# A delta-rule attention with expert layer on one core: weight conversion, first queries and the start of the order are changed

## The chip, the core and the metric

The kernel runs on one core of a Trainium2 chip. The core has a matrix engine (TensorE; PE in the profile, its weight loads PEld), a vector engine (VectorE, DVE), a scalar engine (ScalarE, ACT), a general engine (GpSimd, POOL) and a queue engine (SyncE, SP) that issues transfers. The metric is the device time of one execution in microseconds; a comparison states medians over several runs.

## What is computed

Two steps, the second fed by the first. The first is a recurrence over 768 positions for 4 x 8 = 32 heads of 48 channels, the second a two-layer network over the 3072 resulting rows:

```python
k_n = k / (norm(k) + 1e-06)
for t in range(S):
    y[t] = q[t] @ state
    v_old = state.T @ k_n[t]
    state = state + beta[t] * outer(k_n[t], v[t] - v_old)
h = y @ w_in                       # 384 -> 2048
g = h * tanh(softplus(h))
out = g @ w_out                    # 2048 -> 384
```

q, k, v and beta are float32. The two weight matrices are float64.

## The kernel before

The recurrence is cut into 12 chunks of 64 positions. Within a chunk the products of keys with keys (the "gram") are formed, a triangular system is solved, and the chunk's outputs and the next state follow from small products. The names of the stages are those of the tiles in the profile.

- `early(g)` prepares two chunks at a time. Keys are loaded into `ksrc`, turned in 32x32 blocks by VectorE (`kt`, L408), multiplied (`pg`, L425), masked into `d` (L433) and turned again (`gt`, L451). Then come the norms (`root`, L464), the scaling with beta (L493) and the solve by forward steps, two VectorE operations each (L514, L515). Between the scaling and the end of the solve, GpSimd sets the diagonal of `gt` to one (L504). For the first two pairs of chunks (`split`) the solve covers blocks of 16 in 14 steps, and two products, `ma` (L557) and `mb` (L568), put the halves together. `tu` (L526), `tt` (L528) and `tn` (L576) are turned copies of the solution.
- `s_a` and `s_b` (tiles `ta`, `tb`) join the two 32-blocks of a chunk. `s_gq` multiplies keys and queries, and from chunk 1 on also keys and state (`gq`); VectorE masks the result (L713). `s_z` gives the corrected values (`pz`), `s_y` the outputs (`py`) and the next state (`ps`). All of their products are issued at L590. Each runs twice a chunk, for the two halves h of the heads.
- `turn_q` brings the queries of a chunk, loaded in pieces into `qsrc`, to the layout of the products: two VectorE block transposes for each half (L685). The working tiles `xx` hold state, queries, keys and an identity block; the identity blocks are copied there by VectorE (L278).
- `turn` transposes the outputs (`xt`, L799) and splits them into a high and a low part. `moe(n)` runs the network for chunk n: eight times an `up` product group (`h`, L824, 18 products of 256 columns), the activation on ScalarE (L839, L840, L841) and a `down` group (`acc`, L834, 12 products of 384 columns).
- `convert` turns each of 28 tiles of float64 weights, called parts, from pairs of 32-bit words to a high and a low 32-bit part. For each: ScalarE scales the upper word (L354); GpSimd writes the sign bit over the upper word (L358, two operations in one instruction, compare and multiply) and clamps (L361); VectorE joins in the remaining bits with two operations (L365); ScalarE rounds to the high part (L374); TensorE subtracts it for 24 of the parts (L379, L381) and ScalarE writes the low part (L383), for the others VectorE does both (L385). The temporaries come from the buffers `g`, `e`, `w` and two spare tiles, in the order of `TEMPS`.

The order is made when the kernel is built. Each piece of work is an `op` with an engine, an estimated duration, a priority (lower is earlier), the ops that it follows and the buffers that it holds. `Plan.run` walks forward in estimated time and picks, of what can start soonest, the op of the lowest priority; each engine then executes its instructions in that order. The priorities are set by constants (`SOON`, `E1`, `CV0` and others at L855). `Plan.feed` models how PE's instructions arrive. Semaphores are set by the framework from the data that the instructions share.

At the start SP loads keys, beta, three parts, the queries, two parts, values and keys again, then the other parts; a part from the sixth on waits until the one five before it was scaled (`AHEAD`, L898). `keep_warm` (L868) runs 76 products of zeros on PE before the first keys arrive.

Of the kernel before, what the change touches and what calls it, by code (L numbers as in the profile page):

```python
# [44 lines left out]
class Plan:  # L45
# [6 lines left out]
    THERE, PACKET, ASK, TAKES = 448, 256, 320, 4.0  # L52
# [12 lines left out]
    def feed(self, t, took, words, there, done):  # L65

        rate, left = words / took, words
        while True:
            while done is not None and done <= t:
                there += self.PACKET  # L70
                done = done + self.TAKES if there <= self.ASK else None
            if done is None and there <= self.ASK:
                done = t + self.TAKES
# [12 lines left out]
    def run(self):  # L86
# [12 lines left out]
        def when(o):  # L99
# [15 lines left out]
            if o.words:  # L115
                t = max(t, free["PE"])
                t = max(t, self.feed(t, o.took, o.words, there, due)[0] - o.took)
# [3 lines left out]
        while todo:  # L121
# [20 lines left out]
            if o.words:  # L142
                _, there, due = self.feed(t, o.took, o.words, there, due)
# [27 lines left out]
def kernel(  # L171
# [16 lines left out]
    P = 128  # L188
# [52 lines left out]
    def clear(engine, r0, *ts):  # L241
        for t in ts:
# [5 lines left out]
               op("POOL", 1.0, -100, lambda: [clear(nc.gpsimd, r0, qsrc) for r0 in (32, 96)])]  # L248
# [15 lines left out]
    made = op("POOL", 4.0, -200, constants, bufs=[ident0])  # L264
# [9 lines left out]

    def beside(t):
        for hh in range(2):
            r = slice(64 - 64 * hh, 128 - 64 * hh)
            nc.vector.tensor_copy(t[r, :, hh, D + C:], bcast_mid(ident[r, r.start:r.start + D], PB))  # L278

    eyes = [op("DVE", 0.6, -60, lambda t=t: beside(t), eyer) for t in xx]  # L280
# [5 lines left out]
    def load_src(dst, src, n, prio, *after, engine="SP"):  # L286
# [12 lines left out]
        return made  # L299

# [32 lines left out]
    def convert(k, got):  # L333
# [23 lines left out]
        def sign():  # L357
            nc.gpsimd.tensor_scalar(words()[:, :, 1], a(), 0.0, -2.0 ** 31, op0=ALU.is_lt, op1=ALU.mult)  # L358
# [8 lines left out]
        o = op("POOL", 0.1 + 0.6 * u, prio, sign, o, bufs=held)  # L367
        o = op("POOL", 0.1 + 0.6 * u, prio, clamp, o, bufs=held)
# [25 lines left out]

    kts, ats, nes, tns, vts, yys, ktd, tnd, ned, ttd = {}, {}, {}, {}, {}, {}, {}, {}, {}, {}
    mas = {}
    last_kt, last_s, solves, zs = {}, {}, {}, {}

    def early(g, at):
# [3 lines left out]
        for t2 in range(2):  # L403
# [23 lines left out]
            m = op("PE", 1.5 if g else 1.8, at(0.1 + 0.03 * t2), gram, ktd[n], bufs=[kt, *ps, dt, am], words=256)  # L427
# [76 lines left out]
        o = op("POOL", 0.15, at(0.26), lambda: nc.gpsimd.memset(gf()[:, ::33], 1.0), o, bufs=[gr])  # L504
        for j in range(1, sz - 1):
# [11 lines left out]
            o = op("DVE", 2 * (0.142 + nb_ * m * j * 0.00132), at(0.3 + 0.6 * j / sz), step, o, bufs=[gr, pr])  # L517
        tn = tns[g] = buf("tn", [P, 2, NP, 32], f"tn{g}")
# [143 lines left out]
    loaded, qdn, vdn, sdn, ydn, gdn, zdn, ptr = {}, {}, {}, {}, {}, {}, {}, {}  # L662
# [17 lines left out]
    def turn_q(n, h, prio, got):  # L680
# [6 lines left out]
        qdn[n, h] = op("DVE", 1.46, prio, turn, *got, cleared[4], ydn.get((n - 1, h)), gdn.get((n - 1, h)))  # L687

    def s_gq(n, h):
# [35 lines left out]
        return Stage(0.9 if n else 1.0, 64, products, [qdn[n, h], ktd[n], vdn[n, h], *sdn.get((n - 1, h), ())], [kt, *pg], outs)  # L725
# [137 lines left out]


    zero, warm = buf("e", [P, 512], "zero"), buf("h", [P, 512], "warm")
    o = op("DVE", 0.5, -230, lambda: nc.vector.memset(zero(), 0.0), bufs=[zero])

    def keep_warm():  # L868
        zb = zero().bitcast(BF16)
        for i in range(76):  # L870
            nc.tensor.matmul(warm()[0:32, 0:32] if i < 68 else warm(), zb[:, 0:32 if i < 68 else P], zb[:, :32 if i < 68 else 512],
                             start=True, stop=True)

    op("PE", 5.0, -210, keep_warm, o, bufs=[zero, warm], words=152)
# [7 lines left out]
    def loads(m, prio):  # L882
        for k in todo[:m]:
            kind, i = parts[k]
            got[k] = op("SP", 0.62, prio + 0.001 * k, lambda kind=kind, i=i: load_w(kind, i),
                        kb=1.25 if kind == "i" else 0.95)
        del todo[:m]

    loads(3, -99.5)
    q0 = load_src(qsrc, qq, 0, -99.4)  # L890
    loads(2, -99.3)
    for h in range(2):
        v0 = load_v(0, h, -99.2)
# [22 lines left out]
    mas[1].after += [ydn[0, h] for h in range(2)]  # L916
    for h in range(2):
# [46 lines left out]

    with tc.manual_schedule():
# [32 lines left out]
```

## Time and profile before

| | us |
|---|---|
| median of 3 runs | 646.54 |
| range of the runs | 645.41 to 646.61 |
| the profiled execution | 643.59 |
| its span | 641.8 |
| busy: PE, PEld | 591.0, 550.7 |
| busy: DVE, ACT, POOL | 423.1, 286.0, 150.4 |

The profile comes from one execution. Its span runs from the first to the last recorded event and lies 1.8 us below that execution's own time. Busy times count instructions in execution, so that a line of 92% for PE still says nothing of what PE waited for in a given stretch; the views by stretch, by line and in order of time do. The granted clock is the share of TensorE's full clock that the throttle allowed.

### The profile page before, as it was taken

To read this page: it belongs to the slowest core of one execution; us is meant where nothing else is said; L and a number is where in the kernel's file an instruction comes from. 1 tells how busy PE (TensorE), PEld (TensorE's weight loads), DVE (VectorE), ACT (ScalarE), POOL (GpSimd) and SP (SyncE) were. 2 spreads that over 40 slices of the span, in tenths; PEclk is the share of its full clock that TensorE was granted. 3 is DMA by queue.
4 is the path that set the end of the run, shared out by engine and by line. 5 is a ranking of instruction groups with operands and counts; after the bars stand their busy time and mean duration, and the time that the engine had idled before them with its cause. 6 is when DMAs were issued, how large, how long until landed. Compare 5 with 4: busy or idle time off the path is not lost.

```text
span 641.8 us, 23122 instructions
## 1 busy us (share of the span) xinstructions
PE 591.0 (92%) x10204; PEld 550.7 (86%) x10204; DVE 423.1 (66%) x888; ACT 286.0 (45%) x611; POOL 150.4 (23%) x140
## 2 busy tenths in 40 slices
PE   6049887988999999999999999999999999999996
PEld 4047666867989999999999999999999999999996
DVE  6859699887369984589893499864799932431110
ACT  2116764654553446444446533454433464343322
POOL 6992998795001001010020010010010100000000
PEclk9557989899999999999999999999999999999999
DMA  7886376002331314413115213133123121010001
GB/s 160 205 198 163 53 154 218 14 15 32 64 50 19 66 23 60 68 27 56 30 33 88 35 26 64 26 46 59 27 33 55 27 39 27 15 26 2 19 7 25
DMA packets 160932, 37.77 MB, mean 59 GB/s; under 512 B 154176, under 2 KB 157248, under 8 KB 160832
## 3 DMA queue, kind: packets, MB, share of 16 engines
q1 hardware_dynamic: 156160, 35.85, 28.7%
q8 instruction: 80, 1.31, 0.8%
q10 hardware_dynamic: 4672, 0.44, 0.5%
q14 instruction: 20, 0.16, 0.1%
HBM read 31.56 MB, written 4.72 MB: 57 GB/s over the span
## 4 chain that ended last, share of the span: by engine, by line
PE 79%; DVE 6%; POOL 4%; issue 2%; ACT 1%; POOLq 0%; DVEq 0%
PE h L824 31%; PE acc L834 30%; PE py L590 4%; PE gq L590 2%; PE pz L590 2%; PE ps L590 2%; PE pg L425 2%; POOL ri L358 1%; PE xt L799 1%; PE tb L590 1%; PE ta L590 1%; DVE mi L365 1%; POOL ro L358 1%; POOL mi L361 1%; DVE spare L365 1%
## 5 line engine op out<-in xcount | busy, mean ns | idle before, releaser
L824 PE MATMUL h<-x,wi 128*128 128x256 f32 x1728 | 226.4, 285 | 0.8 <-DVE x L803 0.8
L834 PE MATMUL acc<-wo,g 128*128 128x384 f32 x1152 | 223.7, 343 | 1.6 <-DVE g L841 1.6
L824 PEld LDWEIGHTS h<-x,wi 128*128 128x128 f32 x1728 | 215.3, 189 | 4.6 <-DVE x L803 1.0
L834 PEld LDWEIGHTS acc<-wo,g 128*128 128x128 f32 x1152 | 199.7, 189 | 4.9 <-DVE g L841 1.9
L841 DVE TENSOR_TENSOR g<-e,g 128x512 fp32r<-128x512 f32 x96 | 66.8, 696 | 118.0 <-ACT g L840 117.8
L839 ACT ACTIVATE e<-h 128x512 f32<-128x512 f32 x96 | 57.4, 598 | 172.0 <-PE h L824 153.5
L840 ACT CAST g<-e 128x512 fp32r<-128x512 f32 x96 | 59.7, 622 | 2.6
L515 DVE TENSOR_TENSOR gt<-gt,pr 128x84 f32<-128x84 f32 (+14 forms) x148 | 53.7, 363 | 5.1
L677 POOL TENSOR_TENSOR vt<-vt,ne 128x384 f32<-128x384 f32 x24 | 21.8, 921 | 137.8 <-DVE gt L515 46.8
L514 DVE TENSOR_TENSOR pr<-gt 128x84 f32<-128x84 f32 (+14 forms) x148 | 51.5, 348 | 3.2
L590 PEld LDWEIGHTS py<-xx 128*64 128x64 f32 x768 | 37.5, 142 | 5.7 <-issue 4.7
L713 DVE TENSOR_TENSOR xx<-gq,amask 64x256 f32<-64x256 f32 x96 | 40.5, 422 | 1.7
L590 PE MATMUL py<-xx 128*64 128x48 f32 x768 | 41.2, 228 | 0.4 <-issue 0.4
L504 POOL MEMSET gt<- 128x32 f32 x6 | 0.9, 158 | 166.0 <-DVE gt L493 166.0
L685 DVE STREAM_TRANSPOSE xx<-qsrc 64x512 f32<-64x512 f32 x48 | 33.9, 706 | 6.9 <-PE ps L590 3.7
L590 PE MATMUL ps<-xx 128*48 128x48 f32 x704 | 36.4, 208 | 1.2 <-issue 1.2
L706 DVE TENSOR_TENSOR vt<-vt,gq 64x192 f32<-64x192 f32 (+1 forms) x66 | 23.3, 352 | 19.6 <-PE gq L590 18.9
L779 ACT COPY yy<-py 128x384 f32<-128x384 f32 x24 | 11.5, 479 | 46.8 <-PE py L590 30.2
L609 ACT COPY xx<-pz 64x192 f32<-64x192 f32 x92 | 28.8, 313 | 7.7 <-PE pz L590 6.6
L590 PEld LDWEIGHTS ps<-xx 128*48 128x48 f32 x704 | 30.3, 125 | 2.0 <-issue 1.3
L590 PE MATMUL gq<-xx,kt 64*64 64x112 f32 (+1 forms) x768 | 31.0, 268 | 0.6 <-DVE at L632 0.6
L590 PE MATMUL pz<-vt,tt 64*64 64x48 f32 x768 | 27.8, 224 | 0.5 <-ACT tt L609 0.5
(113 smaller groups left out, 666.0 us busy)
## 6 DMA issues: line engine op xcount, KB each, us to landing
ri<-in_moe_w_in_dram SPq DMA_DIRECT2D x12, 512.0 KB, 6.4
ro<-in_moe_w_out_dram SPq DMA_DIRECT2D x16, 384.0 KB
vt<-in_v_dram SPq DMA_DIRECT2D x48, 96.0 KB, 5.7
xx<-in_k_dram SPq DMA_DIRECT2D x48, 96.0 KB, 3.0
out_dram<-o SPq DMA_DIRECT2D x48, 96.0 KB, 2.9
qsrc<-in_q_dram SPq DMA_DIRECT2D x48, 64.0 KB, 2.7
ksrc<-in_k_dram SPq DMA_DIRECT2D x44, 64.0 KB, 2.7
qsrc<-in_q_dram SPq DMA_DIRECT2D x48, 32.0 KB, 3.1
```

The costliest lines, as they stand in the source:

```text
L514: nc.vector.tensor_tensor(out=pv, in0=nj, in1=xj, op=ALU.mult)
L515: nc.vector.tensor_tensor(out=below, in0=below, in1=pv, op=ALU.add)
L590: nc.tensor.matmul(*a, start=True, stop=True)
L609: (nc.scalar.copy if e == "ACT" else nc.vector.tensor_copy)(out=a, in_=b)
L685: nc.vector.transpose(xx[h][r, :, hh, D:D + C], src)
L706: nc.vector.tensor_tensor(out=vt()[r, p4, :], in0=vt()[r, p4, :], in1=pg[h4]()[i, :, 0:D], op=ALU.subtract)
L713: nc.vector.tensor_tensor(out=x[r, p4, hh, D:D + C], in0=pg[h4]()[i, :, d:], in1=bcast_mid(amask[i], 4), op=ALU.mult)
L824: nc.tensor.matmul(h()[:, f2, :], wt["i", f * P // WI * NCH + c][:, i2, f0:f0 + P], x[:, c, :], start=(i == 0), stop=(i == 3 * NCH - 1))
L834: nc.tensor.matmul(acc[t]()[:, :DM], gg()[:, a, f2, ts_], wt["o", f][:, i2, :], start=(f == 0 and i == 0), stop=(f == NF - 1 and i == 2))
L839: m = op("ACT", 0.58, prio + 0.1, lambda e=e, h=h: nc.scalar.activation(e(), h(), AF.Mish, scale=-1.0), m, bufs=[h, e])
L840: m = op("ACT", 0.58, prio + 0.1, lambda e=e, gg=gg: nc.scalar.copy(out=gg()[:, 0], in_=e()), m, bufs=[e, gg])
L841: m = op("DVE", 0.7, prio + 0.1, lambda e=e, gg=gg: nc.vector.tensor_tensor(out=gg()[:, 1], in0=e(), in1=gg()[:, 0], op=ALU.subtract), m, ...
```

## The change

The conversion: the sign becomes one operation, the scaled number times zero, written as a float whose bits are the sign alone. The clamp now comes before it, and one clamp in four (parts k with k % 4 = 3) runs on VectorE.

```diff
         def sign():
-            nc.gpsimd.tensor_scalar(words()[:, :, 1], a(), 0.0, -2.0 ** 31, op0=ALU.is_lt, op1=ALU.mult)
+            nc.gpsimd.tensor_scalar(words()[:, :, 1].bitcast(F32), a(), 0.0, None, op0=ALU.mult)
-        def clamp():
-            nc.gpsimd.tensor_scalar(a(), a(), -F64_MOST * 2.0 ** -112, F64_MOST * 2.0 ** -112, op0=ALU.max, op1=ALU.min)
+        def clamp(engine):
+            engine.tensor_scalar(a(), a(), -F64_MOST * 2.0 ** -112, F64_MOST * 2.0 ** -112, op0=ALU.max, op1=ALU.min)
...
-        o = op("POOL", 0.1 + 0.6 * u, prio, sign, o, bufs=held)
-        o = op("POOL", 0.1 + 0.6 * u, prio, clamp, o, bufs=held)
+        o = op("POOL", 0.25 + 1.72 * u, prio, lambda: clamp(nc.gpsimd), o, bufs=held) if k in CLAMP_POOL else \
+            op("DVE", 0.13 + 0.3 * u, prio, lambda: clamp(nc.vector), o, bufs=held)
+
+        o = op("POOL", 0.15 + 0.9 * u, prio, sign, o, bufs=held)
```

The queries of chunks 0 and 1 are loaded in their own layout by two transfers (in place of eight), turned by products with the identity on TensorE, and copied by ScalarE. The blocks of `xx` that VectorE's transposes filled with zeros are cleared by GpSimd for this; the clearing of `qsrc` moves behind the reading of chunk 1.

```diff
+    def load_q(n, prio, *after):
+        return [op("SP", 0.6, prio, lambda hh=hh: load(qnat[64 * hh:64 * hh + 64], qq[hh, C * n:C * n + C]), *after, kb=0.9)
+                for hh in range(2)]
...
-        qdn[n, h] = op("DVE", 1.46, prio, turn, *got, cleared[4], ydn.get((n - 1, h)), gdn.get((n - 1, h)))
+        if n > 1:
+            qread[n, h] = op("DVE", 1.46, prio, turn, *got, cleared[4], ydn.get((n - 1, h)), gdn.get((n - 1, h)))
+            qdn[n, h] = [qread[n, h]]
+            return
+        ps = buf("ps", [P, PB, C], f"qt{n}_{h}")
+        x = xx[h]
+
+        def products():
+            for p in range(PB):
+                for hh in range(2):
+                    r = slice(64 * hh, 64 * hh + 64)
+                    nc.tensor.matmul(ps()[64 - 64 * hh:64 - 64 * hh + D, p, :], qnat[r, PB * h + p, :], ident[r, r], start=True, stop=True)
+
+        def out(hh):
+            r = slice(64 - 64 * hh, 64 - 64 * hh + D)
+            nc.scalar.copy(out=x[r, :, hh, D:D + C], in_=ps()[r])
+
+        m = qread[n, h] = op("PE", 1.0, prio, products, *got, eyer, ydn.get((n - 1, h)), gdn.get((n - 1, h)), bufs=[ps], words=64)
+        qdn[n, h] = [op("ACT", 0.62, prio, lambda hh=hh: out(hh), m, cleared[5], ydn.get((n - 1, h)), gdn.get((n - 1, h)), bufs=[ps])
+                     for hh in range(2)]
```

The identity blocks are copied by GpSimd, and the diagonal of the first two pairs is set by VectorE:

```diff
+    def clear_turned():
+        for t in xx:
+            for hh in range(2):
+                r0 = 96 - 64 * hh
+                nc.gpsimd.memset(t[r0:r0 + 32, :, hh, D:D + C], 0.0)
+
+    cleared.append(op("POOL", 2.2, -150, clear_turned))
...
-            nc.vector.tensor_copy(t[r, :, hh, D + C:], bcast_mid(ident[r, r.start:r.start + D], PB))
+            nc.gpsimd.tensor_copy(t[r, :, hh, D + C:], bcast_mid(ident[r, r.start:r.start + D], PB))
...
-        o = op("POOL", 0.15, at(0.26), lambda: nc.gpsimd.memset(gf()[:, ::33], 1.0), o, bufs=[gr])
+        e = "DVE" if split else "POOL"
+        o = op(e, 0.17, at(0.26), lambda: (nc.vector if split else nc.gpsimd).memset(gf()[:, ::33], 1.0), o, bufs=[gr])
```

Products of zeros, besides the 76 at the start, follow steps 2 and 8 of the first solve; their operand moves from the buffer `e` to `x0`.

```diff
+    def keep_warm(n, after, prio, few=0):
+
+        warm = buf("h", [P, 512], "warm")
+
+        def products():
+            for i in range(few + n):
+                m = 32 if i < few else P
+                nc.tensor.matmul(warm()[0:m, 0:4 * m], zero()[:, 0:m], zero()[:, 0:4 * m], start=True, stop=True)
+
+        op("PE", 0.03 * few + 0.4 * n, prio, products, after, bufs=[warm, zerob], words=2 * (few + n))
+
+    WARM = {2: 2, 8: 12}
+    keep_warm(8, o, -210, few=68)
...
             o = op("DVE", 2 * (0.142 + nb_ * m * j * 0.00132), at(0.3 + 0.6 * j / sz), step, o, bufs=[gr, pr])
+            if g == 0 and j in WARM:
+                keep_warm(WARM[j], o, -96)
```

The loads at the start come in another order: queries, values and keys of chunk 0 first, then eleven parts after the second gram, the others after the output product of chunk 0. `AHEAD` is gone.

```diff
-    loads(3, -99.5)
-    q0 = load_src(qsrc, qq, 0, -99.4)
-    loads(2, -99.3)
+    q0 = load_q(0, -99.5)
     for h in range(2):
-        v0 = load_v(0, h, -99.2)
+        v0 = load_v(0, h, -99.4)
         scale_v(0, h, -95, *v0)
-        kxd[0, h] = load_k(0, h, -99.1)
+        kxd[0, h] = load_k(0, h, -99.3)
+    loads(FIRST, -99.2, grams[1])
     loads(28, -99.0)
...
-    for k in range(AHEAD, len(parts)):
-        got[k].after.append(copied[k - AHEAD])
...
+    for k in range(FIRST, len(parts)):
+        got[k].after.append(ydn[0, 1])
```

The rest concerns the plan: other estimates for some durations (GpSimd's above all), another model of PE's instruction supply in `feed`, other priorities, and a low part by TensorE for 25 of the parts in place of 24.

```diff
-    SOON, SOON1, E1, EG, ES, LATE1, LATE = -0.13, 0.007, 0.17, -0.226, 1.8, 0.251, -0.137
-    E1S, LAG, PRIO_XT, CV0, CV1, G1A, XA = 0.646, 2.1, 0.479, -0.25, 1.238, 0.908, 0.14
-    LO_PE = range(24)
-    AHEAD = 5
+    SOON, SOON1, E1, EG, ES, LATE1, LATE = -0.13, 0.377, 0.281, -0.715, 2.034, 0.016, 0.173
+    E1S, LAG, PRIO_XT, CV0, CV1, G1A, XA = 0.898, 2.266, 0.735, -0.411, 1.156, 0.891, -0.134
+    LO_PE = range(25)
+    FIRST = 11
+    CLAMP_POOL = [k for k in range(len(parts)) if k % 4 < 3]
```

More of the change, by code (lines that the diff above doesn't have):

```diff
@@ L63, in op, with feed @@
         return o
-    def feed(self, t, took, words, there, done):
+    def feed(self, t, took, words, there, done, line):
         rate, left = words / took, words
         while True:
[L69 to L73, printed above, removed]
+            if done is not None and done <= t:
+                there, done = there + self.PACKET, None
+            if done is None and there <= self.ASK and left > 0:
+                done = t + self.TAKES + max(0.0, line - t)
             if left <= 0:
@@ L116, in when @@
                 t = max(t, free["PE"])
-                t = max(t, self.feed(t, o.took, o.words, there, due)[0] - o.took)
+                t = max(t, self.feed(t, o.took, o.words, there, due, line)[0] - o.took)
             return t
@@ L142, in run @@
             if o.words:
-                _, there, due = self.feed(t, o.took, o.words, there, due)
+                _, there, due = self.feed(t, o.took, o.words, there, due, line)
             if o.kb:
@@ L247 @@
                op("POOL", 0.5, -219, lambda: clear(nc.gpsimd, 96, ksrc1()), bufs=[ksrc1]),
-               op("POOL", 1.0, -100, lambda: [clear(nc.gpsimd, r0, qsrc) for r0 in (32, 96)])]
+               op("POOL", 1.3, 0.5, lambda: [clear(nc.gpsimd, r0, qsrc) for r0 in (32, 96)])]
+    qnat = qsrc.rearrange("p a b c -> p (a b c)")[:, :NP * D].rearrange("p (a d) -> p a d", d=D)
     def constants():
@@ L262, in constants @@
                                     channel_multiplier=-1)
-    made = op("POOL", 4.0, -200, constants, bufs=[ident0])
+    made = op("POOL", 2.9, -200, constants, bufs=[ident0])
     eyer = op("DVE", 0.3, -98, lambda: nc.vector.tensor_copy(identr, ident0()[:, 0:P]), made, bufs=[ident0])
@@ L277, in beside @@
             r = slice(64 - 64 * hh, 128 - 64 * hh)
-            nc.vector.tensor_copy(t[r, :, hh, D + C:], bcast_mid(ident[r, r.start:r.start + D], PB))
-    eyes = [op("DVE", 0.6, -60, lambda t=t: beside(t), eyer) for t in xx]
+            nc.gpsimd.tensor_copy(t[r, :, hh, D + C:], bcast_mid(ident[r, r.start:r.start + D], PB))
+    eyes = [op("POOL", 1.3, -60, lambda t=t: beside(t), eyer) for t in xx]
     def load(dst, src, queue="SP"):
@@ L392, in sides, with zero @@
         return [(slice(64 * i, 64 * i + 64), slice(64 - 64 * i, 128 - 64 * i)) for i in range(2)]
+    zerob = buf("x0", [P, NCH * UT], "zero")
+    def zero():
+        return zerob().bitcast(BF16)
+    o = op("DVE", 0.3, -230, lambda: nc.vector.memset(zero()[:, 0:512], 0.0), bufs=[zerob])
+    def keep_warm(n, after, prio, few=0):
[7 more added lines that the diff above has]
+    keep_warm(8, o, -210, few=68)
     kts, ats, nes, tns, vts, yys, ktd, tnd, ned, ttd = {}, {}, {}, {}, {}, {}, {}, {}, {}, {}
-    mas = {}
+    mas, grams = {}, {}
     last_kt, last_s, solves, zs = {}, {}, {}, {}
@@ L723, in outs @@
                          for h4 in range(2)]
-        return Stage(0.9 if n else 1.0, 64, products, [qdn[n, h], ktd[n], vdn[n, h], *sdn.get((n - 1, h), ())], [kt, *pg], outs)
+        return Stage(0.9 if n else 1.0, 64, products, [*qdn[n, h], ktd[n], vdn[n, h], *sdn.get((n - 1, h), ())], [kt, *pg], outs)
     def s_z(n, h):
@@ L862, in PRIO_CV @@
         return CV0 + CV1 * k / 28
[L865 to L874, printed above, removed]
     betas = load_beta()
@@ L963 @@
             solves[n // 2 + 1].after.append(m)
+    cleared[4].after += [qread[1, h] for h in range(2)]
     with tc.manual_schedule():
```

13 lines of the change are left out of this document (7 added, 6 removed).

## The prediction

> **What bounds the kernel now.** First the page (span and slices), then busy time by stretch, to see where the slack lies. The windows' columns are start:end, length, then busy us and instruction count of PE, PEld, DVE, ACT and POOL, the granted clock, the DMA share and GB/s.
>
> ```profile
> span 641.8 us, 23122 instructions
> POOL 6992998795001001010020010010010100000000
> ```
> ```profile
> 0.00:35.00 35.00, 9.89 (x332) 7.03 (x332) 26.00 (x63) 7.38 (x13) 28.28 (x40) 0.75 0.83 197
> 35.00:160.00 125.00, 105.68 (x2438) 87.06 (x2439) 101.66 (x192) 66.98 (x143) 96.00 (x65) 0.89 0.44 100
> 160.00:642.00 482.00, 475.44 (x7436) 456.65 (x7434) 295.44 (x635) 211.62 (x456) 26.13 (x37) 1.00 0.23 38
> ```
>
> From 160 us on PE is busy 475.4 of 482 us and POOL nearly idle: there the products set the end, and nothing in this change makes them fewer. So a gain is the amount by which the state of 160 us is reached sooner. Until then PE stands idle 25.1 + 19.3 us, at a mean clock of 0.75 and 0.89.
>
> The first 66 us are a chain from the first keys to the first expert product, as the timelines of PE and DVE show (start, duration, instruction, and in brackets the idle time before it and what ended it):
>
> ```profile
> 35.26 1.90 PE L557 MATMUL ma<-tu,d 16*32 16x16 f32 x128 [21.67 <-DVE tu L526]
> 41.42 1.68 PE L568 MATMUL mb<-tt,ym 32*32 32x16 f32 x110 [3.26 <-issue]
> 48.68 1.42 PE L590 MATMUL tb<-at,tn 32*32 32x32 f32 x64
> 50.61 2.49 PE L590 MATMUL pz<-vt,tt 64*64 64x48 f32 x64 [0.52 <-ACT tt L609]
> 53.03 3.03 PE L590 MATMUL py<-xx 128*64 128x48 f32 x64
> 66.56 2.30 PE L824 MATMUL h<-x,wi 128*128 128x256 f32 x18
> ```
> ```profile
> 7.26 3.12 DVE L278 COPY xx<-identr 64x384 f32<-64x384 f32 x4
> 10.30 1.22 DVE L408 STREAM_TRANSPOSE kt<-ksrc 128x1024 f32<-128x1024 f32 x1
> 32.72 1.27 DVE L520 TENSOR_TENSOR gt<-gt,bp 128x512 f32<-128x512 f32 x1 [1.70 <-POOL gt L504]
> 36.93 1.44 DVE L685 STREAM_TRANSPOSE xx<-qsrc 64x512 f32<-64x512 f32 x2
> 43.15 0.42 DVE L573 TENSOR_TENSOR tt<-tt,mb 128x256 f32<-128x256 f32 x1 [4.77 <-PE mb L568]
> 47.52 3.52 DVE L713 TENSOR_TENSOR xx<-gq,amask 64x256 f32<-64x256 f32 x8
> ```
>
> PE waits 21.67 us for the solve on DVE, then runs ma, mb, tb, pz and py with gaps between them; the first y is there at 56.06, the first expert product (h) starts at 66.56. From 60 to 160 us the weights are converted while all engines are nearly full:
>
> ```profile
> 60.00:160.00 100.00, 87.19 (x1750) 71.22 (x1739) 83.79 (x159) 59.50 (x126) 82.08 (x54) 0.97 0.37 88
> ```
> ```profile
> 62.10 1.92 POOL L358 TENSOR_SCALAR ro<-mo 128x384 int32<-128x384 f32 x1 [12.63 <-PE loi L381]
> ```
>
> The second row shows that POOL had stood idle for 12.63 us before that stretch: its temporaries were all held until PE and DVE came to the weights. The next three rows, busy time of one line over 0 to 160 us, are the sign (L358), the clamp (L361) and the two joins (L365):
>
> ```profile
> 0.00:160.00 160.00, 52.32 (x28) 0.86 0.53 121
> 0.00:160.00 160.00, 49.05 (x28) 0.86 0.53 121
> 0.00:160.00 160.00, 37.67 (x56) 0.86 0.53 121
> ```
>
> There are 28 parts (tiles of weights). Each costs POOL 1.87 us of sign and 1.75 us of clamp, and DVE 1.35 us for its two joins.
>
> **The change, part by part.** Times are against the profiled execution, 643.59 us: its span of 641.8 and 1.8 around it. The runs have a median of 646.54, 2.95 above it; the sum is a difference and I take it from that median.
>
> *Identity blocks to POOL.* The four copies (L278, 3.12 us) stand on DVE between the first and the second key transpose. How early could the second start? Its last keys leave on ACT's queue by 5.88 us and take 2.9 us:
>
> ```profile
> 0.84 5.04 ACTq L284 DMA_DIRECT2D ksrc<-in_k_dram  x8
> ```
> ```profile
> ksrc<-in_k_dram ACTq DMA_DIRECT2D x4, 32.0 KB, 2.9
> ```
>
> so about 8.8 where it is 10.30 now. **-1.5**, between 0 and -3.1. On POOL the copies and four more memsets lie in its idle time before the first weight. Only the SP loads of k into xx wait for them, and behind these the weight loads in SP's queue; the weights now also wait for the second gram. I expect them to leave about 3 us later than now, which costs nothing while POOL's first nine parts end before the chain does.
>
> *Diagonal memset to DVE (first two groups).* It waits 1.70 us behind the signs in POOL's queue; its own time is
>
> ```profile
> 32.53 0.16 POOL L504 MEMSET gt<- 128x32 f32 x1
> ```
>
> On DVE it costs about the same: **-1.5**, -1.0 at the least.
>
> *Products of zeros during the solve.* Two after step 2 and twelve after step 8. What they can win is the clock from ma to py. The same products at full clock, later in the trace:
>
> ```profile
> 58.98 1.26 PE L557 MATMUL ma<-tu,d 16*32 16x16 f32 x128
> 150.33 1.26 PE L568 MATMUL mb<-tt,ym 32*32 32x16 f32 x128
> 73.49 0.75 PE L590 MATMUL tb<-at,tn 32*32 32x32 f32 x64
> 585.70 0.68 PE L590 MATMUL pz<-vt,tt 64*64 64x48 f32 x32
> 592.88 1.14 PE L590 MATMUL py<-xx 128*64 128x48 f32 x32
> ```
>
> ma 0.64 shorter; mb 1.68 x 128/110 = 1.95 to 1.26, 0.7; tb 0.67 and ta, of the same count and size, as much; pz 2.49 to 2 x 0.68, 1.13; py 3.03 to 2 x 1.14, 0.75. Together **-4.6**, or 0 if the clock stays low. How the clock moves:
>
> ```profile
> 17.00:18.00 1.00, 0.00 (x0) 0.00 (x0) 0.91 (x3) 0.00 (x0) 1.00 (x1) 0.82 0.14 24
> 55.00:56.00 1.00, 1.00 (x33) 0.94 (x31) 0.96 (x2) 0.97 (x2) 0.00 (x0) 0.91 0.76 154
> 48.36:51.77 3.41, 2.81 (x104) 2.32 (x100) 3.21 (x9) 0.72 (x2) 1.04 (x2) 0.50 0.55 63
> 51.77:55.18 3.41, 3.41 (x86) 3.32 (x83) 3.22 (x8) 1.41 (x5) 0.00 (x0) 0.50 0.32 54
> 82.48:85.90 3.42, 1.56 (x129) 1.46 (x130) 3.32 (x6) 1.30 (x4) 3.26 (x3) 1.00 0.99 267
> 86.00:87.00 1.00, 1.00 (x3) 0.55 (x2) 1.00 (x3) 0.29 (x1) 1.00 (x1) 0.50 1.03 349
> ```
> ```profile
> L871 PE MATMUL warm<-zero 128*128 128x512 bf16 x8 | 3.6, 631 | 0.0
> ```
>
> A microsecond with a mean of 0.82 fell to 0.5 at 17.64, one with 0.91 rose at 55.18. After 3.4 us with PE 82% busy (48.36 on) it did not rise, after the next, fully busy, it did; after 3.4 us at 46% (82.48 on) it was low again. Eight products of the same size at the kernel's start take 3.6 us together (last row), 0.45 each, so twelve fill 5.4 us without a gap, and by the solve's own rows they end about 1 us ahead of ma: enough for one full stretch of 3.4 us in many cases, not in all. I take the gain, and keep the other case as a rival.
>
> The Trainium skill, page "TensorE: Matmul & The Clock Gate", Part 1, says that the clock is gated by a free-running window of 4096 cycles, 3.4 us, and that where the first products fall in it is chance. The trace agrees: 55.18 - 17.64 is 37.54 us, eleven times 3.41. By that rule alone a gapless 5.4 us holds a whole window in six of ten phases, and the sum would then be -4.6 in one execution and nearer 0 in the next.
>
> *Weight loads held back: eleven until the second gram, seventeen until the first y.* Ahead of mb, PE waits 3.26 us for nothing that the profile shows. PE's instructions come over a DMA queue of their own, through engines that weight loads keep full:
>
> ```profile
> q8 instruction: 80, 1.31, 0.8%
> ```
> ```profile
> ri<-in_moe_w_in_dram SPq DMA_DIRECT2D x12, 512.0 KB, 6.4
> ```
>
> Eleven parts are 5.1 MB: at the 197 GB/s of the first 35 us they last 26 us, past mb; at twice that, when short runs are out of the way, half as long. Between 0 and -3.3 I take **-2.0**. The other seventeen then start near 45 us and take 6.4 us each to land, several at a time; POOL still has parts of the eleven to do.
>
> *First queries by PE and ACT.* Four turns of 1.44 us leave DVE (two of them for chunk 1). PE gets 16 small products and ACT two copies for each, in idle time of both. The query products (gq) then no longer wait for the solve, and the masking (3.52 us on DVE) can fall into the 4.77 us in which DVE waits for mb. tb starts at 48.68 because gq is ahead of it on PE; at's copies are done where the masking begins, 47.52. **-1.2**; 0 to -2.4.
>
> So y(0) is there at 56.06 - (1.5 + 1.5 + 4.6 + 2.0 + 1.2) = 45.3.
>
> *From y(0) to the first expert product*: 10.5 us now, in which DVE does the joins of the first parts and PE the low halves. DVE has 2.9 us less of turns, can place joins in its gaps, and POOL no longer stops for lack of buffers as early. **-3**, between 0 and -7.
>
> *Sign by one operation, a quarter of the clamps on DVE.* The new sign is a one-operation TENSOR_SCALAR, which the trace lacks. Below stands a copy, above the two-operation form (1.87):
>
> ```profile
> L545 POOL COPY tt<-tt 32x512 f32<-32x512 f32 x24 | 15.9, 663 | 31.3 <-DVE tt L528 23.2 <-DVE tt L573 7.1
> ```
>
> I take half of the two-operation form, 0.95. POOL then has 28 x 0.95 + 21 x 1.75 = 63 us in place of 101; DVE gets seven clamps, whose nearest row is a join of the same size (0.67); I take 0.5, since a clamp reads one tensor: 3.5 us. The Trainium skill, "GPSIMD Engine Reference", section 3.1, puts a body of at most two operations at 1.03 cycles an element; by that a sign of 512 elements is an estimated 0.44 us and POOL's sum 49; no run here shows it. POOL was 82% busy in 60 to 160 and is not the limit after. What is late next is DVE (84%) or PE (87%): PE can gain at most its 12.8 us of idle time. I take **-5**, well under half, since the two have to be full together; 0 to -13.
>
> *Other order.* From 160 us on PE has 6.6 us of idle time, most of it the end's drain; I cost the new order there at nothing. The cover is PE's own queue; were it gone, each lost us is a us.
>
> Sum: 10.8 + 3 + 5 = **18.8 us**. Span 623.0, the profiled time 624.8, the runs 646.54 - 18.8 = **627.7**.
>
> **The rivals.**
> 1. *The clock stays low to py.* For it: one window at 82% did not raise it. Against: 5 us without a gap. 632.3. Chance 0.20.
> 2. *DVE becomes the bound.* After the first solve (36.93) DVE does 99.7 us of work by 160; less 5.8 of turns, plus 3.5 of clamps, 97.4. If it packs these no better than now (101.66 of 125, 81%), 120 us from 33.9 (36.93 - 3.0) give 154, a gain of 6: 640.5. For it: DVE waits little in that stretch. Against: part of its idle time was waiting for POOL and mb. 0.14.
> 3. *The sign in one operation is no shorter*, so that part does not do what it says: POOL keeps 52 + 37 us, the -5 and a third of the -3 go: 633.7. Against: every element meets one operation less. 0.07.
> 4. *PE is packed full*: g at -13, the wait before h at -7: 627.7 - 8 - 4 = 615.7. 0.12.
> 5. *Slower: the held loads starve the experts.* Seventeen parts land from about 51 us on and go through four temporaries. Now twenty parts take 62 to 150, 4.4 us each. From 5.9 us a part on, (152 - 51) / 17, the conversion ends later than today; at 6.5 PE loses some 9 us: 655. For it: each part crosses ACT, POOL, DVE, ACT, PE and ACT again. Against: POOL's share falls from 3.6 to about 2.3 us. 0.05.
>
> The forecast, gains of 14 to 24 us, has 0.42. The range 612 to 641 holds the forecast, rivals 1 and 3, most of 2 and 4, and leaves out 5 and the outer ends of 2 and 4, some 0.15. About 0.2% (1.3 us) is what a measurement of this kernel tells from no change: faster 0.93, same 0.02 (the far end of rival 2), slower 0.05.
>
> **What would show it.** In the changed profile: the second key transpose near 8.8; no POOL wait ahead of L520; clock 1.0 at ma; no issue gap ahead of mb; py's end near 45; the first h near 52; POOL's sign near 0.95; the last sign well before 150; PE full from about 140. Wrong would be a clock of 0.5 up to py, a sign near 1.9, or PE waiting on weight tiles after 60 us.

## The result and the profile after

The changed kernel takes 634.85 us (median of 4 runs, 634.05 to 636.15) where the kernel before takes 646.57: a ratio of 0.9825, 95% interval 0.9805 to 0.9845. The profiled execution took 634.87 us, span 633.2. That is at the median, while the profiled execution of before was 3 us under its own, so the traces differ by 8.6 us and the medians by 11.7. Line numbers from here on are those of the changed kernel.

Busy time by stretch of the kernel after (columns as before: PE, PEld, DVE, ACT, POOL, clock, DMA share, GB/s):

```profile
0.00:35.00 35.00, 19.31 (x471) 15.73 (x474) 24.87 (x62) 9.87 (x17) 21.61 (x40) 0.86 0.81 213
35.00:160.00 125.00, 112.68 (x2368) 92.08 (x2369) 95.64 (x188) 72.14 (x153) 79.67 (x61) 0.92 0.44 102
```

Between 35 and 160 us PE is busy 7 us more than before, and POOL 16 us less. The chain up to the first expert product, from the timelines of PE and of DVE:

```profile
35.60 1.91 PE L597 MATMUL ma<-tu,d 16*32 16x16 f32 x128 [11.71 <-DVE xx L772]
38.00 0.29 PE L608 MATMUL mb<-tt,ym 32*32 32x16 f32 x3 [0.49 <-ACT ym L601]
39.81 1.90 PE L608 MATMUL mb<-tt,ym 32*32 32x16 f32 x125 [1.53 <-issue]
...
43.54 1.07 PE L630 MATMUL ta<-tt,at 32*32 32x32 f32 x61 [1.00 <-issue]
...
46.97 1.08 PE L630 MATMUL tb<-at,tn 32*32 32x32 f32 x64
...
49.94 1.15 PE L630 MATMUL pz<-vt,tt 64*64 64x48 f32 x64
...
52.07 2.07 PE L630 MATMUL py<-xx 128*64 128x48 f32 x64
...
59.87 2.30 PE L883 MATMUL h<-x,wi 128*128 128x256 f32 x18
```
```profile
8.59 1.25 DVE L445 STREAM_TRANSPOSE kt<-ksrc 128x1024 f32<-128x1024 f32 x1 [1.77 <-DMA betaT<-in_beta_dram]
...
21.00 0.09 DVE L542 MEMSET gt<- 128x32 f32 x1
...
27.54 0.87 DVE L553 TENSOR_TENSOR gt<-gt,pr 128x88 f32<-128x88 f32 x1
...
30.74 0.98 DVE L560 TENSOR_TENSOR gt<-gt,bp 128x512 f32<-128x512 f32 x1
31.83 1.12 DVE L566 STREAM_TRANSPOSE tu<-gt 128x512 f32<-128x512 f32 x1
32.85 1.91 DVE L568 STREAM_TRANSPOSE tt<-gt 128x1024 f32<-128x1024 f32 x1
34.61 3.49 DVE L772 TENSOR_TENSOR xx<-gq,amask 64x256 f32<-64x256 f32 x8
```

The second key transpose starts at 8.59, and the wait for POOL ahead of L560 is gone. The solve is done at 32.95 (tu, 31.83 + 1.12). But ma starts 2.65 us after that (35.60): the row of ma names the masking of gq (L772) as what ended its wait. ma writes one of the four buffers "ps" in PSUM, the memory to which products are written, and the early gq now holds all four until it is masked. The first y is there at 54.14 (52.07 + 2.07; before 56.06), the first expert product at 59.87 (before 66.56). So of the 8.6 us, 1.9 are won up to y(0), 4.8 from there to the first h, and 1.9 after it.

Where the products of zeros went, from the timeline of PE and the windows:

```profile
19.33 0.38 PE L424 MATMUL warm<-zero 128*128 128x512 bf16 x1 [0.16 <-issue]
19.64 1.55 PE L630 MATMUL gq<-xx,kt 64*64 64x64 f32 x64
21.34 2.54 PE L424 MATMUL warm<-zero 128*128 128x512 bf16 x11 [0.16 <-issue]
```
```profile
28.00:29.00 1.00, 0.00 (x0) 0.00 (x0) 0.96 (x2) 0.66 (x1) 1.00 (x2) 0.94 1.05 424
29.00:30.00 1.00, 0.00 (x0) 0.00 (x0) 0.93 (x3) 0.54 (x1) 1.00 (x2) 0.50 1.01 406
49.00:50.00 1.00, 1.00 (x7) 0.39 (x6) 0.94 (x3) 0.00 (x0) 1.00 (x2) 0.82 0.06 16
```

The twelve (eleven have a record) run right behind gq and end at 23.9, before step 8 does (25.6). "After step 8" holds in the planner's list alone. The products share no data with the step, so no semaphore makes PE wait for it. PE is then idle for 11.7 us, the clock falls near 28.9 and comes back near 49.4, just ahead of pz (49.94).

The conversion: busy time of the sign (L371) and of the clamp (L374, DVE and POOL) over 0 to 160 us, and the first POOL conversion in its timeline:

```profile
0.00:160.00 160.00, 39.87 (x28) 0.90 0.52 126
0.00:160.00 160.00, 3.56 (x7) 36.99 (x21) 0.90 0.52 126
```
```profile
25.59 1.92 POOL L374 TENSOR_SCALAR mi<-mi 128x512 f32<-128x512 f32 x1 [8.98 <-ACT mi L367]
...
131.66 1.57 POOL L371 TENSOR_SCALAR ro<-mo 128x384 f32<-128x384 f32 x1 [7.03 <-DVE mo L374]
```

A sign now takes 1.42 us (39.87 / 28), three quarters of the 1.87 before and not half; POOL's signs and clamps sum to 76.9 us (before 101.4). A clamp is 1.76 us on POOL and 0.51 on DVE. POOL starts its first conversion 10.8 us later than before (14.8) and its last one 17 us earlier (before at 149). The start is late because the weights are: SP issues their first loads at 20.43, and at 8.86 before (the first row is before's):

```profile
8.86 2.30 SPq L284 DMA_DIRECT2D ri<-in_moe_w_in_dram  x3
20.43 1.57 SPq L293 DMA_DIRECT2D ri<-in_moe_w_in_dram  x3
```

### The profile page after: what moved, and what is told of

The parts are those of the page before. It is cut to its first block, busy times and chain, and to the rows that moved or that the text cites. A ratio compares the mean times of both kernels' runs of the same rounds, so it can differ in the third digit from the quotient of the medians.

```text
span 633.2 us, 23406 instructions
## 1 busy us (share of the span) xinstructions
PE 600.3 (95%) x10346; PEld 557.9 (88%) x10349; DVE 417.6 (66%) x884; ACT 290.8 (46%) x620; POOL 131.0 (21%) x139
## 4 chain that ended last, share of the span: by engine, by line
PE 80%; DVE 8%; DMA 3%; POOL 3%; issue 2%; SPq 2%; ACT 1%; DVEq 0%; POOLq 0%; ACTq 0%
PE acc L893 31%; PE h L883 30%; PE py L630 3%; PE gq L630 3%; PE pg L462 2%; DMA ri<-in_moe_w_in_dram 2%; PE ps L630 2%; SPq L293 2%; PE pz L630 2%; PE ta L630 1%; PE warm L424 1%; PE tb L630 1%; DVE gt L553 1%; DVE pr L552 1%; PE xt L858 1%
## 5 line engine op out<-in xcount | busy, mean ns | idle before, releaser
L552 DVE TENSOR_TENSOR pr<-gt 128x84 f32<-128x84 f32 (+14 forms) x148 | 54.6, 369 | 3.4
L553 DVE TENSOR_TENSOR gt<-gt,pr 128x84 f32<-128x84 f32 (+14 forms) x148 | 50.4, 341 | 5.1
L772 DVE TENSOR_TENSOR xx<-gq,amask 64x256 f32<-64x256 f32 x96 | 40.5, 422 | 1.7
L585 POOL COPY tt<-tt 32x512 f32<-32x512 f32 x24 | 17.4, 723 | 109.8 <-DVE tt L568 92.2
L630 PE MATMUL py<-xx 128*64 128x48 f32 x768 | 39.7, 224 | 0.0
L717 POOL TENSOR_TENSOR vt<-vt,ne 128x384 f32<-128x384 f32 x24 | 22.5, 956 | 52.9 <-DMA vt<-in_v_dram 52.6
L725 DVE STREAM_TRANSPOSE xx<-qsrc 64x512 f32<-64x512 f32 x40 | 28.2, 706 | 4.3 <-PE ps L630 2.5
L838 ACT COPY yy<-py 128x384 f32<-128x384 f32 x24 | 11.5, 480 | 38.2 <-PE py L630 23.0
```

The costliest lines, as they stand in the source:

```text
L552: nc.vector.tensor_tensor(out=pv, in0=nj, in1=xj, op=ALU.mult)
L553: nc.vector.tensor_tensor(out=below, in0=below, in1=pv, op=ALU.add)
L630: nc.tensor.matmul(*a, start=True, stop=True)
L725: nc.vector.transpose(xx[h][r, :, hh, D:D + C], src)
L772: nc.vector.tensor_tensor(out=x[r, p4, hh, D:D + C], in0=pg[h4]()[i, :, d:], in1=bcast_mid(amask[i], 4), op=ALU.mult)
```

## The experiments

Twelve kernels were run, each timed against the kernel before on the same chip. In the first eight the order of the work is that of the changed kernel (in one, of before), written out as a list, so that an edit can't make the planner lay out another; experiments 2 and 5 move entries of that list. In the next three the planner lays out its own; the last has the list again. The changed kernel stands at 0.9825.

**1. The products of zeros left out.**

```diff
-        op("PE", ..., products, after, bufs=[warm, zerob], ...)
+        op("PE", ..., products if few else (lambda: None), after, bufs=[warm, zerob] if few else [], ...)
```

> The fourteen products of zeros beside the solve left out (the opening ones stay), the order of everything else as in the changed kernel. Theory A (they ran too early: they ended at 23.9 us, before the eighth step was done, and the clock was down again at 29, six microseconds before ma): nothing is lost, the ratio to the kernel before stays at 0.9825 within 0.002, ma still takes 1.91 us. Rival (they carried the clock for the chain up to y(0), and it would be longer without them): 3 to 5 us more, ratio 0.987 to 0.990.

Measured: 634.80 us, ratio 0.9828 (0.9805 to 0.9851). The profiled execution took 1,942 us, so its trace says nothing of the other four (633.61 to 635.75 us), and whether ma still takes 1.91 us is not shown. The fourteen products bring nothing that the intervals, some 2 us either way, would let through; the rival's 3 to 5 us are out.

**2. The products made to wait for step 12.** The twelve stand behind that step in the list, and a write of one column of their operand, by VectorE, holds them there.

```diff
         def products():
+            if n > 8:
+                nc.vector.memset(zerob()[:, 0:1], 0.0)
```

> The twelve products moved behind the twelfth step in the order and made to wait for it, by a write of one column of the zero tile on VectorE that stands behind that step. Theory A: they start near 28.5 and end near 33, the granted clock is 1.0 at ma, ma falls from 1.91 to about 1.0 us, mb from 2.2 to about 1.1, tb from 1.08 to about 0.55, and the time falls by 2 to 4 us (ratio 0.976 to 0.980). Rival (issue gaps and the masking set the pace there, so the rate of the products is hidden): under 1 us, ratio 0.981 to 0.984.

Measured: 635.53 us, ratio 0.9846 (0.9822 to 0.9871). The timeline of PE and two windows of this kernel:

```profile
30.80 5.30 PE L425 MATMUL warm<-zero 128*128 128x512 bf16 x12 [10.78 <-DVE zero L422]
36.52 1.28 PE L597 MATMUL ma<-tu,d 16*32 16x16 f32 x128 [0.41 <-DVE xx L772]
38.29 0.23 PE L608 MATMUL mb<-tt,ym 32*32 32x16 f32 x3 [0.49 <-ACT ym L601]
40.51 1.89 PE L608 MATMUL mb<-tt,ym 32*32 32x16 f32 x125 [1.99 <-issue]
```
```profile
36.00:40.00 4.00, 1.61 (x132) 1.35 (x132) 3.60 (x8) 0.38 (x1) 3.92 (x4) 0.92 0.70 105
40.00:45.00 5.00, 2.42 (x145) 2.18 (x148) 2.31 (x4) 0.63 (x1) 4.92 (x5) 0.50 0.30 30
```

The wait works: the clock is up at ma, which takes 1.28 us and not 1.91. Yet nothing is won. mb stands still no shorter (1.99 us; 1.53 in the changed kernel, but 1.99 also in experiment 6, whose edit leaves this chain alone), PE is busy 1.61 of 4 us, and the clock is down again when mb goes on. So theory A is right in that the products ran too early, and wrong in what that cost; its rival came nearest.

**3. PSUM buffers of their own for ma and mb.**

```diff
-        ps = buf("ps", [P, NP, 16], f"ma{n}")
+        ps = half(buf("acc0", [P, 512], f"ma{n}")) if n == 0 else buf("ps", [P, NP, 16], f"ma{n}")
...
-        ps2 = buf("ps", [P, NP, 16], f"mb{n}")
+        ps2 = half(buf("acc1", [P, 512], f"mb{n}")) if n == 0 else buf("ps", [P, NP, 16], f"mb{n}")
```

> ma and mb of the first chunk get two buffers in PSUM that lie free then, in place of those that gq holds until it is masked. Theory B (the early gq turned the wait for its masking into one of ma): ma starts near 33.0 and not at 35.6, y(0) ends about 2.6 us earlier, and the time falls by 1 to 2.6 us (ratio 0.9785 to 0.981). Rival (what follows ma, the add behind the maskings on VectorE or the conversion, is late anyway): ma moves and the time stays, ratio 0.9815 to 0.9845.

Measured: 633.38 us, ratio 0.9823 (0.9797 to 0.9849). The timeline of PE:

```profile
34.04 2.18 PE L597 MATMUL ma<-tu,d 16*32 16x16 f32 x128 [11.35 <-DVE tu L566]
...
39.31 1.90 PE L608 MATMUL mb<-tt,ym 32*32 32x16 f32 x125 [2.32 <-issue]
...
43.58 1.07 PE L630 MATMUL ta<-tt,at 32*32 32x32 f32 x61 [1.55 <-issue]
```

ma waits for tu alone and starts 1.56 us earlier, but the stop ahead of mb grows to 2.32 us and that in ta to 1.55; ta goes on at 43.58, where it did before the edit (43.54), and y(0) ends 0.4 us earlier (53.78) and not 2.6. What takes the gain back is "issue", not the engine that theory B's rival named.

**4. The old conversion in the changed kernel.** The two-operation sign, and all 28 clamps on GpSimd.

```diff
-            nc.gpsimd.tensor_scalar(words()[:, :, 1].bitcast(F32), a(), 0.0, None, op0=ALU.mult)
+            nc.gpsimd.tensor_scalar(words()[:, :, 1], a(), 0.0, -2.0 ** 31, op0=ALU.is_lt, op1=ALU.mult)
...
-    CLAMP_POOL = [k for k in range(len(parts)) if k % 4 < 3]
+    CLAMP_POOL = range(28)
```

> The changed kernel with the old conversion alone: sign by two operations, all 28 clamps on GpSimd, order as changed. Theory D (the stretch from 60 to 150 us is still led by GpSimd, whose sum goes back from 76.9 to about 101 us): 5 to 12 us more, ratio 0.990 to 1.001. Rival (another engine leads there already, and the shorter sign brought little): within 2 us of the changed kernel, ratio 0.980 to 0.986.

Measured: 650.95 us, ratio 1.0075 (1.0053 to 1.0096): 16 us more, beyond theory D's 12, and slower than before the change. Its stretch from 60 to 150 us, and what PE waited for from 60 us on (total, times, longest):

```profile
60.00:150.00 90.00, 76.86 (x1326) 60.50 (x1325) 60.76 (x115) 54.34 (x117) 79.39 (x51) 0.91 0.38 102
```
```profile
PE loi L394 <- DVE mi L378: 4.0, 2, 3.7
...
PE loo L394 <- DVE spare L378: 2.5, 1, 2.5
PE loi L394 <- DVE spare L378: 2.3, 2, 1.3
```

POOL is busy 79.4 of 90 us. PE waits 8.8 us in these rows for weights that come through POOL; in the changed kernel the rows of these names add up to 4.4. The first h starts 3.8 us later (63.65), and PE's clock has a mean of 0.91 (0.99 in the changed kernel). How the 16 us divide among these was not separated. In this order the conversion is worth 16 us, and the rest of the change by itself costs 5.

**5. The weights earlier.** Three loads ahead of the queries, their scales ahead of the copies of the turned queries, and the other seventeen loads ahead of the values of chunk 1; only the list of the order is edited.

> The changed kernel, its order touched in three places: the first three weight loads leave ahead of the queries, values and key copies of the first chunk, ScalarE scales them ahead of the copies of the turned queries, and the seventeen later loads leave ahead of the values of the second chunk. Theory C (the 11.6 us by which the first weights leave later cost most of what the shorter conversion brings): GpSimd's first conversion starts near 15 and not at 25.6 us, its last sign falls from 131.7 to about 125, and the time falls by 3 to 6 us (ratio 0.973 to 0.978). Rival (what starts earlier collides with the solve on VectorE, and the second batch is limited by the buffers): within 1.5 us, ratio 0.980 to 0.985.

Measured: 640.50 us, ratio 0.9907 (0.9874 to 0.9940), 5 us more than the changed kernel. The timeline of PE:

```profile
19.07 0.42 PE L738 MATMUL qt<-identr,qsrc 64*48 64x64 f32 x2 [5.04 <-DMA qsrc<-in_q_dram]
...
58.66 2.07 PE L630 MATMUL py<-xx 128*64 128x48 f32 x64
```

POOL's first conversion starts at 17.67, but the queries come later (PE waits 5.0 us for them), ma starts at 37.27, and y(0) ends at 60.73 where it ended at 54.14, with the DMA engines full up to 60 us (share 0.96 from 35 us on, 0.58 in the changed kernel). The weights go ahead of loads that the first y needs. Theory C fell in this form; which of the two moves does the harm was not separated.

**6. The clamps of the last twenty parts on VectorE.**

```diff
-    CLAMP_POOL = [k for k in range(len(parts)) if k % 4 < 3]
+    CLAMP_POOL = [k for k in range(8) if k % 4 < 3]
```

> The changed kernel with the clamps of the last twenty parts all on VectorE (15 more of them there; the first eight parts as they are). Theory D (GpSimd still leads the conversion between 60 and 150 us): its sum falls by about 26 us, VectorE takes on about 7, and the time falls by 2 to 5 us (ratio 0.975 to 0.980). Rival (VectorE, 45.6 of 50 us busy from 100 to 150, is the bound there): no change to 3 us more, ratio 0.982 to 0.988.

Measured: 631.51 us, ratio 0.9778 (0.9750 to 0.9806). The stretch from 60 to 150 us, in the changed kernel and then with this edit:

```profile
60.00:150.00 90.00, 81.82 (x1411) 67.47 (x1409) 74.68 (x147) 56.63 (x119) 58.68 (x45) 0.99 0.40 102
```
```profile
60.00:150.00 90.00, 84.36 (x1547) 71.07 (x1546) 78.76 (x163) 58.15 (x123) 36.75 (x31) 0.98 0.42 104
```

POOL has 22 us less, DVE only 4 more, and PE is busy 2.5 us more in the same time; its waits for weights there (for the low halves, loi and loo) fall from 4.7 us to 1.0. So theory D's forecast of the time holds: POOL's clamps still stood ahead of weights that PE waited for. But POOL was not the fullest engine there; it was busy 58.7 of 90 us, less than DVE and PE.

**7. The new conversion alone in the kernel before**, in the order of before: experiment 4's edit the other way round, the clamp ahead of the sign.

> The kernel before, in its own order, with the new conversion alone: sign by one operation, every fourth clamp on VectorE. The reverse test cost 16 us, so if parts add up (theory: the rest of the change is a loss of some 4 to 5 us, by the late weights) it lands near 630 us, ratio 0.972 to 0.979, below the changed kernel. Rival (the conversion pays that much only where the weights come late, and the rest of the change is neutral or a gain by itself): 632 to 640 us, ratio 0.980 to 0.990.

Measured: 641.36 us, ratio 0.9932 (0.9907 to 0.9957): 5.4 us and not 16. The parts don't add up; the rival came nearest (its range ended at 640 us).

**8. Eight tiny products more, ahead of the twelve.**

```diff
-                keep_warm(WARM[j], o, -96)
+                keep_warm(WARM[j], o, -96, few=8 if WARM[j] > 8 else 0)
```

> The changed kernel with eight more tiny products of zeros (32 by 128) ahead of the twelve, which run while TensorE waits anyway. The stops marked issue fall on every 128th matmul (number 94 or 95 of each 128, in before, the changed kernel and three experiments), and each ends 3.5 to 5.3 us after the one 128 earlier was issued: theory E is that TensorE's instructions arrive in blocks of 128 matmuls with their weight loads. Then the stop ahead of the fourth product of mb moves to mb's last few, ending near the same time (41.5), the stop of 1.0 us in ta goes, and y(0) ends about 1.3 us earlier; the time falls by 0.5 to 1.5 us (ratio 0.980 to 0.982). Rival (the stops come from the transfers of weights or from what stands there in the kernel): both stay at the fourth product of mb and of ta, ratio 0.9825 within 0.002.

Measured: 635.85 us, ratio 0.9840 (0.9813 to 0.9867). The timeline of PE:

```profile
36.06 1.89 PE L597 MATMUL ma<-tu,d 16*32 16x16 f32 x124 [13.35 <-DVE xx L772]
39.76 0.29 PE L597 MATMUL ma<-tu,d 16*32 16x16 f32 x4 [1.81 <-issue]
40.54 1.88 PE L608 MATMUL mb<-tt,ym 32*32 32x16 f32 x123 [0.48 <-ACT ym L601]
43.59 0.29 PE L608 MATMUL mb<-tt,ym 32*32 32x16 f32 x5 [1.17 <-issue]
44.40 1.08 PE L630 MATMUL ta<-tt,at 32*32 32x32 f32 x64 [0.52 <-DVE tt L613]
```

With eight products more ahead of them, both stops come seven or eight products earlier in the chain (some records are missing): from the fourth of mb to the last four of ma, from the fourth of ta to the last five of mb. So they sit on a count of products and not on a place in the kernel, and the two stand 128 matmuls with their weight loads apart, as in the other kernels with two such stops. Counted from the start (76 products of zeros, 256 of the gram and so on), the first stop comes after product 478 in before, 605 in the changed kernel and 606 here: 94, 93 and 94 past a multiple of 128.

The transfers in the traces show what is waited for. PE's instruction queue, q8 in the page of before, moved 80 packets, 1.31 MB, for 10,204 recorded products: one for each 128. Between the start of ma and the end of a first stop it has one packet, and one more up to the end of the second. In before these packets end at 40.16 and 43.52 us, the stops at 41.42 and 44.87; in the changed kernel at 38.42 and 42.14, the stops at 39.81 and 43.54. Over before, the changed kernel and experiments 2 to 12, every first and second stop ends 1.2 to 1.6 us after such a packet.

What differs is when the first packet starts, and that goes with the load of the DMA engines. The windows are the first 3 us of ma in before and in the changed kernel:

```profile
35.26:38.26 3.00, 2.40 (x146) 2.19 (x147) 2.94 (x3) 0.38 (x1) 2.84 (x3) 0.50 1.11 241
35.60:38.60 3.00, 2.19 (x131) 1.98 (x132) 2.88 (x7) 0.38 (x1) 2.92 (x3) 0.50 1.00 123
```

The packet starts 1.0 to 1.5 us after ma where 92 to 123 GB/s move in these 3 us (the changed kernel, experiments 2, 8 and 11), 2.1 to 2.2 us after it at 135 to 227 GB/s (4, 5 and 6), and 2.5 to 3.9 us at 237 to 391 GB/s (before, 3, 7, 9, 10 and 12). This compares kernels that differ in other things too; no run changed the load alone. So theory E's mechanism holds, and its rival keeps a part: the count says where a stop falls, and the load of transfers goes with how long it is. The forecast of the time failed: the stop fell one block earlier than expected, into ma, the second did not go, and the two did not shrink (2.98 us for 2.53).

**9 to 11. The order alone.** In the kernel before, the planner is told that a sign or a clamp on GpSimd takes 0.7 us for 512 columns, where the rows had 1.95. Experiment 9 corrects that figure and nothing else; 10 and 11 are experiments 7 and 4 with the order laid out anew, under the costs that fit their instructions.

```diff
-        o = op("POOL", 0.1 + 0.6 * u, prio, sign, o, bufs=held)
-        o = op("POOL", 0.1 + 0.6 * u, prio, clamp, o, bufs=held)
+        o = op("POOL", 0.25 + 1.72 * u, prio, sign, o, bufs=held)
+        o = op("POOL", 0.25 + 1.72 * u, prio, clamp, o, bufs=held)
```

> The kernel before with not one instruction changed, but its planner told what a sign and a clamp on GpSimd take (0.25 us + 1.72 us for each 512 columns, as the rows have it, in place of 0.1 + 0.6), so that it lays out another order. Theory F (the order is a part of the change with a price of its own, which the prediction set at zero): 3 to 8 us less than before, ratio 0.988 to 0.995. Rival (the order is neutral, the instructions make the difference): within 2 us, ratio 0.997 to 1.003.

> The kernel before with the new conversion (sign by one operation, every fourth clamp on VectorE) as in the reverse test, but its order laid out anew with the new operations' costs. Theory F (in the old order the conversion brought 5.4 us because the engines, which take their work in order, stood at products placed for another conversion): 8 to 13 us less than before, ratio 0.980 to 0.988, most of the whole change's gain. Rival (the early turn of the queries, the held weights and the memset are needed for it): near the 641 us of the old order, ratio 0.990 to 0.995.

> The changed kernel with the old conversion as in the other reverse test, its order laid out anew with the old operations' costs. Theory F: much of the loss of 5 us against before goes, 641 to 647 us, ratio 0.992 to 1.001. Rival (the weights that leave 11.6 us later cost this much in any order, as GpSimd must do the same sum after a later start): 648 to 652 us, ratio 1.003 to 1.009.

Measured (us, ratio to before with its interval):

| instructions | order as in before or after | planner's own order, true costs |
|---|---|---|
| before | 646.6, 1 | 661.71, 1.0240 (1.0208 to 1.0272) |
| before + new conversion | 641.36, 0.9932 | 650.22, 1.0065 (1.0042 to 1.0089) |
| after with old conversion | 650.95, 1.0075 | 645.87, 1.0004 (0.9990 to 1.0018) |
| after | 634.85, 0.9825 | (the same) |

Rows with the same instructions differ by 5 to 16 us. Theory F was right that the order has a price, and wrong about its sign in 9 and 10: true figures made before's planner lay out worse orders; in 11 it came out as forecast. The priorities of before were left as they were, so whether true figures with other priorities would do better is not shown. From the waits of experiment 9's PE (total, times, longest):

```profile
PE ma L557 <- issue: 9.1, 3, 4.9
PE mb L568 <- issue: 4.4, 2, 2.7
...
PE loo L379 <- issue: 2.9, 1, 2.9
```

From 30 us on the stops marked issue add up to 18.3 us there and 12.7 in experiment 10, against 6.3 in before and 2.9 in after. Experiment 9 has 12 us more of them than before and is 15 to 16 us slower; that these waits are the loss is likely, but argued, since a wait taken away came back as another in experiment 3. In the right-hand column the conversion is worth 11.0 us (645.87 - 634.85) and 11.5 (661.71 - 650.22), and the rest of the change 15 to 16 in both. It is one order for each cell, so this is an agreement and no proof.

**12. Clamps on VectorE and the PSUM buffers together.**

> The changed kernel with both edits that helped or did no harm: the clamps of the last twenty parts on VectorE and separate PSUM buffers for ma and mb of the first chunk. Theory D with B: the 3 us of the clamps stay and ma's earlier start adds 0 to 1.5, ratio 0.974 to 0.979. Rival (the stops for TensorE's instruction blocks take back what ma gains, as they did alone): the ratio of the clamps alone, 0.978 within 0.002.

Measured: 630.40 us, ratio 0.9766 (0.9741 to 0.9791), the lowest of all, 4 us under the changed kernel. The ratio lies in both ranges, and from experiment 6 it can't be told apart. The timeline of PE speaks for the rival:

```profile
39.56 1.89 PE L608 MATMUL mb<-tt,ym 32*32 32x16 f32 x125 [3.42 <-issue]
```

ma starts 1.78 us earlier than in experiment 6, and mb goes on only 0.19 us earlier: the stop ahead of it is 3.42 us and not 1.99.

## Why the prediction was right, and where not

The direction and the range held; the forecast gain of 18.8 us was 7 too much. That the range held is in part luck. The traces show 1.9 us of the 10.8 forecast up to y(0), and 8.6 in all; the runs' 11.7 lies 3 us above that, because the profiled execution of before was a quick one. By the prediction's steps, in the order of its sum:

- *Identity blocks to POOL, -1.5; diagonal memset, -1.5.* Right: 10.30 to 8.59 and a wait of 1.70 gone. The solve's steps gave back 1.0 us (21.16 to 30.7, 9.6 us for 8.6), while POOL works beside them: a step of 0.25 us takes 0.87 at 27.54, just after POOL began its L717 (27.48). That POOL is the cause is argued from such coincidences.
- *Products of zeros, -4.6.* **This step failed.** It took "after step 8" for a wait that the hardware keeps. Experiment 1 puts the products at nothing, and experiment 2 shows that even with the wait kept the clock doesn't last to py, since the chain stands still between its products. Rival 1 (0.20, 632.3 us), the clock low to py, describes this best, though by another cause and only as far as pz; by the number alone rival 3 (633.7) lies nearer. pz and py became faster (2.49 to 1.15, 3.03 to 2.07 us), at a clock that came back after PE had been busy without a gap from 43.54 us on, with ta, tb and the low halves of weights. The fall of the clock near 28.9 and its return near 49.4 (from the windows' means of 0.94 and 0.82) lie 20.5 us apart, six times 3.41. That agrees with the Trainium skill, page "TensorE: Matmul & The Clock Gate", Part 1, on its window; the phase, on which the prediction let this term hang, turned out not to matter.
- *Weight loads held back, -2.0.* The stop ahead of mb fell by 1.7 and that in ta rose by 0.3, so the size was near. The cause that it names, transfers that delay PE's instructions, fits the packets of experiment 8, where the first one starts 3.52 us after ma in before and 1.48 in the changed kernel; but no run isolates it, and the prediction missed that a count of 128 products sets where the stops fall. What failed is how long the loads are held: the weights left 11.6 us later (20.43 after 8.86) and not 3.
- *First queries by PE and ACT, -1.2.* Mis-sized: gq left the path as said, and its PSUM buffers came onto it, 2.65 us ahead of ma. Experiment 3 shows that this wait costs nothing by itself, since the next instruction block is then waited for instead.
- *y(0) at 45.3:* 54.14. Of the miss of 8.8 us, 3.3 lie ahead of ma (its wait of 2.65 and the slower steps) and 5.5 between ma and y(0): of the 7.8 us forecast there, pz and py gave 2.3 and the stops 1.5, and some 1.5 went back, with low halves of weights now between ta, tb, pz and py.
- *y(0) to first h, -3:* 4.8; within its bounds. *Sign and clamps, -5:* 1.9 after the first h in the profiled pair. The sign was mis-sized: 1.42 us for 0.95, so POOL's sum is 76.9 for 63, and its clamps still hold weights back, as experiment 6 shows by gaining 3 us from fewer of them. The clamp on DVE was right (0.51 for 0.5). The Trainium skill, "GPSIMD Engine Reference", section 3.1, by which a sign of 512 elements would be an estimated 0.44 us, stands against 1.53 in the row of that size; the measurement decides.
- *Other order, 0.* **This step failed too**, and it can't be seen in the total. The cover that it named (PE's queue from 160 us on) is not where the order acts. Experiments 4, 7 and 9 to 11 put it at 5 to 16 us for the same instructions. In experiment 9 the difference arises before 160 us: from there on PE is still busy for 493.6 us, and for 475.4 in before.

Rival 2 (DVE as the bound) did not happen: DVE took on fifteen more clamps and the time fell. Rival 3 (the sign no shorter) is half true: the sign fell by a quarter. Rival 5 (weights late) showed as its weaker half: the weights did come late, and bringing them forward cost more.

What stays open: how much of the 11.7 us belongs to which part. In the changed order the conversion is worth 16 us, in the old one 5.4, and the parts are defined only together with an order.

## What to carry to other kernels

Ask of each "after" in a program whether data enforce it: work that shares no tile with its predecessor runs as soon as its engine is free. Where engines take their work in order, price the order itself, and test a part both by undoing it and by adding it alone; if the two disagree, as 16 and 5.4 us did here, the order is one thing that can carry the difference. And on a chain of many small products look at what feeds instructions before speeding up the products.

## What the runs showed of the hardware

- TensorE's instructions came in blocks of 128 matmuls with their weight loads, one packet on q8 each (80 packets for 10,204 recorded products in before). In a chain of small products after a wait, the next product ran 1.2 to 1.6 us after its block's packet ended, and 3.4 to 6.7 us after the chain's start or the block before; the 128 products of ma take 1.28 us at full clock. With a faster clock, an earlier start or another phase the two stops added up to 2.98 to 4.69 us (experiments 2, 3, 8 and 12), against 2.53 in the changed kernel and 3.54 in experiment 6, whose chain is the same.
- GpSimd's one-operation TENSOR_SCALAR takes 1.53 us for 128 x 512 where the two-operation one took 1.97, so the second operation adds 0.44. DVE's two-operation clamp takes 0.42 to 0.83 for the same tile (three rows).
- DVE's small steps (0.25 us) took up to 0.87 while GpSimd worked, but most did not: beside GpSimd's clamp of 25.59 to 27.51 one took 0.68 and the next four kept 0.25 to 0.27.
